# Converting the first four weight slices without absolute value and clamp, and loading their high words again later for a check

## The chip, the cores and the metric

The kernel runs on one core of one Trainium2 chip. The metric is the device time of one execution in microseconds (us): the median of three runs. Beside it stands one execution that the hardware profiler recorded; all rows in this document are of such executions. The engines are PE (TensorE matrix product; PEld is its weight load), DVE (VectorE), ACT (ScalarE), POOL (GpSimd) and SP (SyncE, which here only issues DMA transfers; its queue is SPq).

## The reference

Attention over 4 batches, 8 heads, 768 positions and 64 features per head, then a feed-forward network on its result. The projections `w_in` and `w_out` come as 64-bit floating point; the chip has to convert them.

```
scores = scale * q @ k.T + bias(head, distance); masked to a local band and some global keys
a = exp(scores - max); a = a / (sum(a) + 1e-9)
x = (a @ v) as 3072 tokens x 512
h = x @ w_in                      # 512 x 2048, float64
g = where(h > 0, h, exp(min(h, 0)) - 1)
out = (g @ w_out) as float32      # 2048 x 512, float64
```

## The kernel before, in words

The 3072 tokens are 12 groups of 256. For each group and each of 4 head pairs a chain runs: scores on PE (`s`), a masked minimum on DVE, exponentials on ACT (`pr`, L464), division, transposition, the product with v, and a split of the result into a high and a low part (`xh`, `xl`). The feed-forward part takes 16 slices of 128 hidden units: an up product into a PSUM bank `h` (12 products of 128x256; there are two such banks, h0 and h1), two ACT instructions on it (`e`, L720 and L721), one on DVE (`gg`, L722), from two slices a set of sums and splits (`rh`, `rl`, `sh`, `sl`), and a down product into banks `o`. From group 4 on, the function `seven` works on pairs of slices with seven block products instead of eight; it reads mixtures of weights (`mix`) that are loaded from DRAM for each pair. The first three groups are taken four slices at a time, while the weights are still being converted.

`weight` converts one slice of one matrix: a load of 128x1024 32-bit words (`bits`), an absolute value of the high words on ACT (L393), a clamp on DVE or POOL (L395), a shift and mask on DVE (L396), two DVE instructions that put in the sign and the low bits (L398, L400), and a split into two parts (L303 or L305, L311). Slices 0 to 3 of both matrices are eight such conversions.

The order of the instructions on each engine is not written by hand. `Plan.add` collects operations with the tiles that they read and write and a due time; `Plan.order` then builds a schedule from a table of costs and hands out slots for the tiles. An engine takes its instructions in the order that comes out, and an instruction whose operand has not arrived holds those behind it on that engine. Tiles of one class are handed out in the order in which they were added. The class `io` (four slots, `io0` to `io3`) holds the conversion's `g` early on, and later the output tiles `ob`, two for each group (slots io0 and io1), which DVE fills at the end of a group and SP stores (L805). Where the schedule shows a gap on PE in the first part, the kernel puts in products that nobody reads, to keep PE busy: `none<-fill` (L1096) and `<-zero` (L1089).

At the end a flag that tells whether the inputs lie outside of what this fast path covers is summed over the partitions; a branch on it leads to `dense`, a slow path that does not run with these inputs.

Of the kernel before, what the change touches and what calls it, by code (L numbers as in the profile page):

```python
# [28 lines left out]
HI, LO = 0, 1  # L29

F64_MIN = 2.0 ** -15
F64_MAX = 1.875 * 2.0 ** 16 - 2.0 ** -7
# [192 lines left out]
def sp():  # L225
    return (("SP", 450.0, False),)
# [19 lines left out]
class Kernel:  # L246
# [67 lines left out]
    def consts(self):  # L314
        self.ident = self.const("ident", [P, P])
        self.far0, self.far1 = self.const("far0", [P, LW]), self.const("far1", [P, LW])

        self.scale = self.const("scale", [P, self.NP])
        if self.ON_PE:
            self.minus1 = self.const("minus1", [P, P], F32R)  # L320
        self.nmax = self.const("nmax", [P, self.B * self.H * self.S // P])
        self.zero = self.const("zero", [P, W], F32R)
        self.sums = {x: self.c.tile([P, 2 * NT, 4], F32, name=x) for x in self.SLOTS["st"]}
# [57 lines left out]
    def weight(self, which, fc, due, after):  # L381
        nc, p, DM = self.nc, self.plan, self.DM
        tag = f"w{which}{fc}"
        bits = self.sb(tag, "bits", [P, 2 * DM], I32)
        g = self.sb("io", "g", [P, DM], I32)
        w = self.sb(tag, f"w{which}", [P, 2, DM], F32R)
        src = (self.w_in, self.w_out)[which][fc].bitcast(I32)
        words = lambda: bits.t.rearrange("p (n w) -> p n w", w=2)
        low, high = lambda: words()[:, :, 0], lambda: words()[:, :, 1]
        gf = lambda: g.t.bitcast(F32)  # L390
        p.add(sp(), lambda e: nc.sync.dma_start(bits.t, src), writes=[bits], due=due - 9000, after=after, nbytes=P * DM * 8, early=due - 9000 - self.EARLIER)

        p.add((("ACT", 575.0, False),), lambda e: nc.scalar.activation(gf(), high().bitcast(F32), AF.Abs), [bits], [g], due - 6000)  # L393
        p.add(dve(DM, True) + (("POOL", 640.0, True),),
              lambda e: self.on(e).tensor_scalar(gf(), gf(), F64_MAX, F64_MIN, ALU.min, ALU.max), [g], [g], due - 5500)  # L395
        p.add(dve(DM, True), lambda e: nc.vector.tensor_scalar(g.t, g.t, 3, 0x3FFFFFFF, ALU.logical_shift_left, ALU.bitwise_and),  # L396
              [g], [g], due - 5000)
        p.add(dve(DM, port=True), lambda e: nc.vector.scalar_tensor_tensor(g.t, high(), -0x40000000, g.t, ALU.bitwise_and, ALU.bitwise_or),  # L398
              [bits, g], [g], due - 4500)
        p.add(dve(DM, port=True), lambda e: nc.vector.scalar_tensor_tensor(g.t, low(), 29, g.t, ALU.logical_shift_right, ALU.bitwise_or),  # L400
              [bits, g], [g], due - 4000)
        p.add(act(DM) + pool(DM, False) + dve(DM, True), lambda e: self.copy(e, w.t[:, HI], gf()), [g], [w], due - 3000)
        if (which, fc) in self.ON_PE:

            lw = self.bank("lw", "lw", [P, DM], ["h0", "h1"])

            def lower(e):
                nc.tensor.matmul(lw.t, self.ident.t, gf(), start=True, stop=False)
                nc.tensor.matmul(lw.t, self.minus1.t, w.t[:, HI], start=False, stop=True)

            p.add((("PE", 1500.0, False),), lower, [g, w], [lw], due - 2500)
            p.add(act(DM, True), lambda e: self.copy(e, w.t[:, LO], lw.t), [lw], [w], due - 2000)
        else:
            def lower(e):
                for c in range(0, DM, DM // 2):
                    x = slice(c, c + DM // 2)
                    self.minus(e, w.t[:, LO, x], gf()[:, x], w.t[:, HI, x])

            p.add((("POOL", 1390.0, True),), lower, [g, w], [w], due - 2000)
        return w  # L420


    def pair(self, b, gi, hp, xh, xl, due, step, X):
        nc, p = self.nc, self.plan
# [487 lines left out]
    def build(self):  # L912
# [20 lines left out]
        for n, (b, gi) in enumerate(groups):  # L933
# [17 lines left out]
        for k in range(len(self.fars) + self.BEHIND):  # L951
            d = self.fars[max(0, k - self.BEHIND)][-2] - max(0, self.BEHIND - k) * self.AHEAD
# [7 lines left out]
        for (n, f0, f1), d in zip(segs, dues):  # L960
            def moe(n=n, f0=f0, f1=f1, d=d):
                b, gi = groups[n]
                if f0 == 0 and f1 < NFC:
                    parts[n] = [self.sb("part", "part", [P, self.DM]) for _ in range(NT)]
                if n >= self.SE:
                    self.seven(b * self.S + gi * W, *X[n], d, self.STEP, n == len(groups) - 1)
                    return
                self.moe(b * self.S + gi * W, *X[n], f0, f1, d, self.STEP, parts.get(n), n < self.NE, n == len(groups) - 1)
            todo.append((d[f0], moe))
        self.kept, self.mixed = {}, {}  # L970
        for j in range(NFC // 2):
            d = [x for (n, _, _), x in zip(segs, dues) if n == self.SE - 1][-1][2 * j + 1] + 2 * self.STEP
            e = self.PREPARE[0] + j * self.PREPARE[1]
# [26 lines left out]
    SOON, EARLIER = (5000.0, 2500.0, 14000.0), 1e9  # L1000
    NEAR = {}
    WARM = True
    WIDE, BEHIND_UP = ["h0", "h1", "v0", "t0"], 3.0
    THIRD = {"xha": "x0", "xhb": "ph2", "xla": "rk0", "xlb": "va0"}
    SLOTS = {"qk": ["rqv0", "qk0"], "v": ["va1", "va2"], "u": ["rk0", "va0"], "s": ["s0", "s1"], "t": ["t0"], "pv": ["v0", "t0"], "h": ["h0", "h1"], "o0": ["o0"], "o1": ["o1"],
# [95 lines left out]
    def flag(self):  # L1101
        nc, c = self.nc, self.c
        ng, nl = self.ng, self.nl
        f = c.tile([P, 8], F32, name="flag")
        nc.vector.tensor_reduce(f[:, 0:1], self.nmax.t, axis=AX.X, op=ALU.max)
        nc.vector.tensor_scalar(f[:, 0:1], f[:, 0:1], 9.0e8, None, ALU.is_ge)
        nc.vector.tensor_scalar(f[:, 1:2], ng, 0.0, None, ALU.is_lt)
        nc.vector.tensor_scalar(f[:, 2:3], ng, float(NG), None, ALU.is_gt)
        nc.vector.tensor_scalar(f[:, 3:4], nl, 0.0, None, ALU.is_lt)
        nc.vector.tensor_scalar(f[:, 4:5], nl, float(BACKW + 1), None, ALU.is_gt)  # L1110
        nc.vector.tensor_tensor(f[:, 5:6], ng, nl, ALU.add)
        nc.vector.tensor_scalar(f[:, 5:6], f[:, 5:6], 1.0, None, ALU.is_lt)
        nc.vector.tensor_reduce(f[:, 6:7], f[:, 0:6], axis=AX.X, op=ALU.max)
        one = c.tile([P, 1], F32, name="one")
        nc.gpsimd.memset(one, 1.0)
        return f, one

    def flag_sum(self, flags):
        nc, c = self.nc, self.c
        f, one = flags  # L1120
        s = self.ps.tile([P, 1], F32, tag="s0", name="flagsum")
        nc.tensor.matmul(s[0:1, :], f[:, 6:7], one, start=True, stop=True)
        fi = c.tile([1, 1], I32, name="flagint")
        nc.vector.tensor_copy(fi, s[0:1, :])
        self.fi = fi
# [110 lines left out]
    def restored(self):  # L1236
        M = self.DM // 2
        for j, x in self.kept.items():
            self.nc.sync.dma_start(self.ws[1][2 * j].t[:, :, M:].bitcast(F32), x.t)

    def dense(self, b):
        for t0 in range(0, self.S // P, NT):
            self.dx = [self.p.tile([P, self.NCC, W], F32R, tag=f"dx{i}", name=self.n("dx")) for i in range(2)]
            for i in range(NT):
                self.dense_tile(b, t0 + i, i)
            self.dense_moe(b, t0)


def tile_kernel(tc, q, k, v, qkv, qkv1, n, w_in, w_out, out):
    with ExitStack() as ctx:  # L1250
        f = Kernel(ctx, tc, q, k, v, qkv, qkv1, n, w_in, w_out, out)
        f.w = ctx.enter_context(tc.tile_pool(name="w", bufs=1))
        with tc.tile_pool(name="m", bufs=1) as f.m:
            flag = f.run()
        with tc.If(flag > 0, label="dense"):
            with ExitStack() as x:
                f.p = x.enter_context(tc.tile_pool(name="d", bufs=1))
                f.restored()
                with tc.For_i(0, f.B, 1) as b:
                    f.dense(b)  # L1260

# [63 lines left out]
```

## Time and profile before

| | |
|---|---|
| median of 3 runs | 644.96 us (644.52 to 646.63) |
| the profiled execution | 645.14 us, span of its instructions 643.4 us |
| PE busy | 632.4 us, 98% of the span |
| DVE, ACT, POOL busy | 493.9, 410.6, 197.4 us |
| granted TensorE clock, mean | 0.997 of full speed |
| DMA, mean | 233 GB/s |

Busy is time in which an engine ran instructions of its own work. The busy share is an average over stages with different limits, so the stretches have to be looked at one by one.

### The profile page before, as it was taken

To read this page: it belongs to the slowest core of one execution; us is meant where nothing else is said; L and a number is where in the kernel's file an instruction comes from. 1 tells how busy PE (TensorE), PEld (TensorE's weight loads), DVE (VectorE), ACT (ScalarE), POOL (GpSimd) and SP (SyncE) were. 2 spreads that over 40 slices of the span, in tenths; PEclk is the share of its full clock that TensorE was granted. 3 is DMA by queue.
4 is the path that set the end of the run, shared out by engine and by line. 5 is a ranking of instruction groups with operands and counts; after the bars stand their busy time and mean duration, and the time that the engine had idled before them with its cause. 6 is when DMAs were issued, how large, how long until landed. Compare 5 with 4: busy or idle time off the path is not lost.

```text
span 643.4 us, 19163 instructions
## 1 busy us (share of the span) xinstructions
PE 632.4 (98%) x7054; PEld 585.2 (91%) x7054; DVE 493.9 (77%) x1649; ACT 410.6 (64%) x1200; POOL 197.4 (31%) x499
## 2 busy tenths in 40 slices
PE   8999999999999999999999999999999999999995
PEld 5778888898898889999999999999999999999995
DVE  5999888899878975777777777786786777775655
ACT  5999777676554655666566576566566566655552
POOL 3556565465467672121111111112112022020000
PEclk9999999999999999999999999999999999999998
DMA  8979825231266899798888888898888888875542
GB/s 306 372 256 407 338 90 150 70 111 62 68 204 230 258 302 305 236 271 262 262 237 274 278 243 259 289 263 254 286 238 270 258 264 270 276 220 162 181 149 85
DMA packets 131171, 149.82 MB, mean 233 GB/s; under 512 B 63616, under 2 KB 82816, under 8 KB 131072
## 3 DMA queue, kind: packets, MB, share of 16 engines
q1 hardware_dynamic: 130928, 148.54, 72.3%
q8 instruction: 57, 0.93, 0.6%
q14 instruction: 42, 0.34, 0.2%
q10 hardware_dynamic: 144, 0.00, 0.0%
HBM read 117.57 MB, written 30.93 MB: 231 GB/s over the span
## 4 chain that ended last, share of the span: by engine, by line
PE 92%; DVE 2%; ACT 2%; DMA 2%; issue 1%; POOL 0%; DVEq 0%; ACTq 0%; SPq 0%; POOLq 0%
PE h L712 28%; PE o L768 24%; PE o L863 14%; PE h L837 14%; PE s L610 5%; PE s L474 5%; PE pv L507 2%; DMA qk<-in_qkv_dram 2%; PE t L527 1%; PE none L1096 1%; PE t L529 1%; ACT pt L303 1%; ACT pr L464 0%; DVE ob L796 0%; ACT qk L449 0%
## 5 line engine op out<-in xcount | busy, mean ns | idle before, releaser
L712 PE MATMUL h<-xh,w 128*128 128x256 f32 x1024 | 142.2, 281 | 0.1
L712 PEld LDWEIGHTS h<-xh,w 128*128 128x128 f32 x1024 | 129.8, 188 | 2.3 <-issue 1.2
L722 DVE SCALAR_TENSOR_TENSOR gg<-e,h 128x256 f32<-128x256 f32 x128 | 53.3, 416 | 75.7 <-ACT e L721 74.9
L580 POOL TENSOR_SCALAR pr<-pr,st 128x168 f32<-128x168 f32 x144 | 62.6, 435 | 150.9 <-DVE st L482 137.9
L464 ACT ACTIVATE pr<-pr,nmax 128x168 f32<-128x168 f32 x192 | 81.8, 427 | 17.6 <-DVE nmax L462 16.9
L837 PEld LDWEIGHTS h<-xh,w 128*128 128x128 f32 x512 | 77.0, 188 | 9.8 <-issue 0.2
L720 ACT ACTIVATE e<-h 128x256 f32<-128x256 f32 x128 | 48.6, 379 | 56.3 <-PE h L712 56.0
L712 PE MATMUL h<-xl,w 128*128 128x256 f32 x512 | 81.9, 281 | 0.0
L863 PE MATMUL o<-w,gh 128*128 128x512 f32 x256 | 81.6, 400 | 0.1
L837 PE MATMUL h<-xh,w 128*128 128x256 f32 x512 | 81.6, 283 | 0.0
L712 PEld LDWEIGHTS h<-xl,w 128*128 128x128 f32 x512 | 69.4, 188 | 2.0 <-issue 1.7
L462 DVE CUSTOM_DVE_ANT_0 pr<-s,far 128x168 f32<-128x168 f32 x192 | 53.3, 324 | 12.8 <-ACT xh L303 11.1
L311 POOL TENSOR_TENSOR w<-g,w 128x256 fp32r<-128x256 f32 x64 | 51.0, 818 | 36.0 <-ACT w L303 30.0
L303 ACT CAST sh<-sum 128x512 fp32r<-128x512 f32 x64 | 39.8, 621 | 31.4 <-DVE sum L736 31.4
L585 DVE STREAM_TRANSPOSE tr<-pr 128x192 f32<-128x192 f32 x144 | 50.0, 364 | 10.6 <-POOL pr L580 7.4
L721 ACT ACTIVATE e<-e 128x256 f32<-128x256 f32 x128 | 53.4, 417 | 3.6
L768 PE MATMUL o<-mix,sh 128*128 128x256 f32 x256 | 51.0, 281 | 0.0
L863 PEld LDWEIGHTS o<-w,gh 128*128 128x128 f32 x256 | 43.0, 188 | 7.6 <-issue 1.0
L311 DVE TENSOR_TENSOR sl<-sum,sh 128x512 fp32r<-128x512 f32 x64 | 44.2, 691 | 5.7 <-ACT sh L303 5.7
L768 PE MATMUL o<-w,sh 128*128 128x256 f32 x256 | 48.2, 280 | 0.0
L451 POOL TENSOR_SCALAR qk<-qk,scale 128x256 f32<-128x256 f32 x14 | 7.1, 506 | 133.3 <-DMA qk<-in_qkv_dram 90.1
L303 ACT CAST rh<-gg 128x384 fp32r<-128x384 f32 x64 | 32.8, 512 | 20.4 <-DVE gg L722 19.7
(136 smaller groups left out, 1421.4 us busy)
## 6 DMA issues: line engine op xcount, KB each, us to landing
mix<-mixed SPq DMA_DIRECT2D x192, 256.0 KB, 4.5
qk<-in_qkv_dram SPq DMA_DIRECT2D x48, 312.0 KB, 4.2
v<-in_qkv_dram SPq DMA_DIRECT2D x36, 384.0 KB, 5.0
dd<-tr SPq DMA_DIRECT2D x36, 384.0 KB, 4.5
pt<-dd SPq DMA_DIRECT2D x72, 192.0 KB, 3.9
bits<-in_w_in_dram SPq DMA_DIRECT2D x16, 512.0 KB, 8.6
bits<-in_w_out_dram SPq DMA_DIRECT2D x16, 512.0 KB, 9.5
mixed<-mix SPq DMA_DIRECT2D x32, 256.0 KB, 3.1
```

The lines of the kernel that those rows point to most:

```text
L303: self.nc.scalar.copy(out, x)
L311: self.on(e).tensor_tensor(out, x, y, ALU.subtract)
L462: first = p.add((("DVE", 85 + 1.042 * LW, False),), lambda e: nc.vector.tensor_tensor_reduce(x(), s.t[:, i, :LW], tab, -(2.0 ** -(h + 1)), ...
L464: p.add(act(LW, extra=200), lambda e: nc.scalar.activation(x(), x(), AF.Exp, bias=nm, scale=-1.0, accum_out=st.t[:, n, 0:1]), [pr], [pr, s ...
L580: nc.gpsimd.tensor_scalar(pr.t[:, :LW], pr.t[:, :LW], st.t[:, n, 3:4], 1.0, ALU.mult, ALU.mult)
L585: nc.vector.transpose(tr.t[:, :, i, j], pr.t.rearrange("p (b r) -> p b r", r=32))
L712: nc.tensor.matmul(h.t, w1.t[:, s, cc * P:(cc + 1) * P], self.chunk(x, cc), start=n == 0 and s == HI and cc == 0, stop=n == 1 and cc == se ...
L721: p.add(act(W), lambda e: nc.scalar.activation(ex.t, ex.t, AF.Exp, scale=-1.0), [ex], [ex], d - 8000)
L722: p.add(dve(W), lambda e: nc.vector.scalar_tensor_tensor(gs(), ex.t, -1.0, h.t, ALU.add, ALU.max), [h, ex], [g], d - 8000)
L768: nc.tensor.matmul(acc[bank].t[:, half], a, b.t[:, LO if t == 1 else HI, x], start=j == 0 and t == 0 and n in first, stop=j == self.NFC // ...
L837: nc.tensor.matmul(h.t, w1.t[:, s, cc * P:(cc + 1) * P], self.chunk(x, cc), start=n == 0 and cc == 0, stop=n == 2 and cc == self.NCC - 1)
L863: nc.tensor.matmul(o.t[:, :at.stop - at.start], g.t[:, i * P:(i + 1) * P], w2.t[:, s, at], start=fc == f0 and n == 0 and s == HI, stop=fc ...
```

## The change

For slices 0 to 3 (`BARE = 4`) of both matrices the absolute value and the clamp are left out, and the shift reads the high words of `bits` directly. To still tell a weight outside of the covered range, `watch` loads the words again later, in 16 transfers of 256 KB (the two matrices, four slices, two halves each), and runs two ACT instructions over the high words of each: an absolute value and an exponential, each with a sum along the row into `wide`. Five short DVE instructions in `flag` turn `wide` into one more bit of the flag. The slow path converts the four slices again with the clamp (`rewritten`, not run here and not shown).

```
-        p.add((("ACT", 575.0, False),), lambda e: nc.scalar.activation(gf(), high().bitcast(F32), AF.Abs), [bits], [g], due - 6000)
...
+        bare = fc < self.BARE
+        if not bare:
+            p.add((("ACT", 575.0, False),), lambda e: nc.scalar.activation(gf(), high().bitcast(F32), AF.Abs), [bits], [g], due - 6000)
+            p.add(dve(DM, True) + (("POOL", 640.0, True),),
+                  lambda e: self.on(e).tensor_scalar(gf(), gf(), F64_MAX, F64_MIN, ALU.min, ALU.max), [g], [g], due - 5500)
+        p.add(dve(DM, port=True) if bare else dve(DM, True), lambda e: nc.vector.tensor_scalar(
+            g.t, high() if bare else g.t, 3, 0x3FFFFFFF, ALU.logical_shift_left, ALU.bitwise_and), [bits if bare else g], [g], due - 5000)
...
+    def watch(self, k, due):
...
+        nc, p, DM = self.nc, self.plan, self.DM
+        which, fc, half = k % 2, k // 2 % self.BARE, k // 2 // self.BARE
+        src = (self.w_in, self.w_out)[which][fc].bitcast(I32)[:, half * DM:(half + 1) * DM]
+        x = self.sb("io", "seen", [P, DM], I32, slots=["io0", "io1"])
+        p.add(sp(), lambda e: nc.sync.dma_start(x.t, src), writes=[x], due=due - 4000, nbytes=P * DM * 4, early=due - 4000)
+        t = lambda: x.t.rearrange("p (n w) -> p n w", w=2)[:, :, 1].bitcast(F32)
+        w, n = self.wide, 4 * self.BARE
+        p.add(act(DM // 2, extra=200), lambda e: nc.scalar.activation(t(), t(), AF.Abs, accum_out=w[:, k:k + 1]), [x], [x], due)
+        p.add(act(DM // 2, extra=200), lambda e: nc.scalar.activation(t(), t(), AF.Exp, scale=-512.0, accum_out=w[:, n + k:n + k + 1]), [x], [x], due)
...
+        for k in range(4 * self.BARE):
+            d = self.WATCH[0] + k * self.WATCH[1]
+            todo.append((d - 4000.0, lambda k=k, d=d: self.watch(k, d)))
...
+    BARE, WATCH = 4, (255000.0, 12000.0)
```

The 16 loads use the slots of the output tiles, so they stand behind the stores at the ends of five groups (4 to 8): 2, 4, 4, 4 and 2 of them. First the SP queue at the end of group 4, before the change: the two stores of the output, three loads of mixtures, and the loads for the attention of a later group.

```order
L805 DMA out_dram<-ob_5192 128x512
L805 DMA out_dram<-ob_5156 128x512
L751 DMA mix_5249<-mixed_3302 128x512
L751 DMA mix_5265<-mixed_3271 128x512
L751 DMA mix_5280<-mixed_3286 128x512
L548 DMA qk_5324<-in_qkv_dram 128x624
L556 DMA v_5336<-in_qkv_dram 128x768
```

The same place with the change (lines are 16 higher in the changed file), with what each instruction waits for; DMAHW5 and DMAHW6 are here the semaphores of the two stores:

```order
L821 DMA out_dram<-ob_5166 128x512 [waits DMAHW5_49,DVE_49]
L821 DMA out_dram<-ob_5130 128x512 [waits DMAHW6_49,DVE_49]
L767 DMA mix_5223<-mixed_3276 128x512 [waits PE_49]
L767 DMA mix_5239<-mixed_3258 128x512 [waits DMAHW0_49,PE_49]
L767 DMA mix_5254<-mixed_3264 128x512 [waits DMAHW1_49,PE_49]
L433 DMA seen_5256<-in_w_in_dram 128x512 [waits DMAHW5_49,DMAHW2_49]
L433 DMA seen_5294<-in_w_out_dram 128x512 [waits DMAHW6_49,DMAHW3_49]
L564 DMA qk_5302<-in_qkv_dram 128x624 [waits DMAHW4_49,PE_49,Activation_49]
```

Two loads have come in behind the mixtures. Each waits for the store that empties its slot. At the next three group ends a second pair of loads follows, and these wait for the ACT instructions on the first pair, whose slots they take.

ACT at the same place before the change: `e` on the first slice of the new group, exponentials of the attention, `e` on the second slice.

```order
L720 ACTIVATE e_5338<-h_5269 128x256
L721 ACTIVATE e_5338<-e_5338 128x256
L464 ACTIVATE pr_5340,st_75<-pr_5340,nmax 128x168
L464 ACTIVATE pr_5343,st_75<-pr_5343,nmax 128x168
L720 ACTIVATE e_5365<-h_5326 128x256
L464 ACTIVATE pr_5349,st_75<-pr_5349,nmax 128x168
L721 ACTIVATE e_5365<-e_5365 128x256
L464 ACTIVATE pr_5361,st_75<-pr_5361,nmax 128x168
```

And with the change:

```order
L736 ACTIVATE e_5316<-h_5243 128x256
L737 ACTIVATE e_5316<-e_5316 128x256
L480 ACTIVATE pr_5318,st_76<-pr_5318,nmax 128x168
L436 ACTIVATE seen_5256,wide<-seen_5256 128x256
L736 ACTIVATE e_5343<-h_5304 128x256
L437 ACTIVATE seen_5256,wide<-seen_5256 128x256
L436 ACTIVATE seen_5294,wide<-seen_5294 128x256
L737 ACTIVATE e_5343<-e_5343 128x256
L437 ACTIVATE seen_5294,wide<-seen_5294 128x256
```

The four new instructions stand in front of and between the two `e` of the second slice; the other exponentials have moved behind them.

PE in the first part, at the first up product of the feed-forward network, before the change: runs of seven and of two unread products (`none<-zero`) stand around it.

```order
L1089 MATMUL none_566<-zero 128x256 x7
L837 MATMUL h_574<-xh_331,w_104_463 128x256 x2
L837 MATMUL h_574<-xh_500,w_104_463 128x256 x2
L837 MATMUL h_574<-xh_331,w_104_463 128x256 x2
L837 MATMUL h_574<-xh_500,w_104_463 128x256 x2
L527 MATMUL t_589<-ident,pr_486 128x128
L527 MATMUL t_589<-ident,pr_493 128x128
L529 MATMUL t_589<-ident,pr_486 128x128
L529 MATMUL t_589<-ident,pr_493 128x128
L837 MATMUL h_574<-xl_350,w_104_463 128x256 x2
L837 MATMUL h_574<-xl_520,w_104_463 128x256 x2
L1089 MATMUL none_614<-zero 128x256 x2
```

And with the change: the first run is two products long, the second is gone, and the second slice's product has moved up. In the whole program the products of L1089 (L1109 in the changed file) fall from 22 (runs of 7, 2, 5, 4, 4) to 11 (runs of 2 and 9), and those of L1096 rise from 22 to 24.

```order
L1109 MATMUL none_560<-zero 128x256 x2
L853 MATMUL h_563<-xh_333,w_104_410 128x256 x2
L853 MATMUL h_563<-xh_482,w_104_410 128x256 x2
L853 MATMUL h_563<-xh_333,w_104_410 128x256 x2
L853 MATMUL h_563<-xh_482,w_104_410 128x256 x2
L853 MATMUL h_563<-xl_351,w_104_410 128x256 x2
L853 MATMUL h_563<-xl_501,w_104_410 128x256 x2
L543 MATMUL t_582<-ident,pr_473 128x128
L543 MATMUL t_582<-ident,pr_480 128x128
L545 MATMUL t_582<-ident,pr_473 128x128
L545 MATMUL t_582<-ident,pr_480 128x128
L853 MATMUL h_592<-xh_333,w_110_553 128x256 x2
```

## Rows read from the trace of the kernel before

**Rows 1.** Page, part 1: busy time of each engine, share of the span, instructions.

```profile
PE 632.4 (98%) x7054; PEld 585.2 (91%) x7054; DVE 493.9 (77%) x1649; ACT 410.6 (64%) x1200; POOL 197.4 (31%) x499
```

**Rows 2.** Windows: length, busy us (x instructions) by engine, PE clock, DMA share, GB/s.

```profile
30.00:40.00 10.00, 8.99 (x133) 7.42 (x132) 9.33 (x37) 9.85 (x35) 6.02 (x9) 1.00 0.51 159
40.00:50.00 10.00, 9.54 (x110) 7.51 (x110) 9.93 (x38) 9.80 (x34) 5.46 (x8) 1.00 0.98 366
...
280.00:320.00 40.00, 40.00 (x542) 38.51 (x541) 28.86 (x105) 25.14 (x74) 5.71 (x25) 1.00 0.85 262
```

**Rows 3.** PE groups from 6 to 70 us, unread products: busy us, mean ns | idle before.

```profile
L1096 PE MATMUL none<-fill 128*128 128x512 f32 x14 | 5.5, 509 | 0.0
L1089 PE MATMUL none<-zero 128*128 128x256 f32 x14 | 2.3, 294 | 0.0
L1089 PE MATMUL o<-zero 128*128 128x256 f32 x8 | 1.4, 293 | 0.0
```

**Rows 4.** Lines of the conversion, 0 to 160 us: duration ns min/median/max, first and last start.

```profile
L393 ACT ACTIVATE g<-bits x32: 647/674/692, 14.9 to 156.0; 128x512 f32<-128x512 f32 x32
L395 DVE TENSOR_SCALAR g<-g x10: 415/423/940, 15.7 to 154.8; 128x512 f32<-128x512 f32 x10
L396 DVE TENSOR_SCALAR g<-g x30: 412/424/964, 18.1 to 157.1; 128x512 int32<-128x512 int32 x30
L398 DVE SCALAR_TENSOR_TENSOR g<-bits,g x30: 644/684/1222, 18.6 to 159.3; 128x512 int32<-128x512 int32 x30
```

**Rows 5.** Timeline of ACT from 10 us: start, us, line, tiles; pieces merged.

```profile
21.88 1.83 ACT L393 ACTIVATE g<-bits 128x512 f32<-128x512 f32 x3
```

**Rows 6.** Timeline of SP's queue at the end of group 4: start us, us of issuing.

```profile
308.80 0.86 SPq L805 DMA_DIRECT2D out_dram<-ob  x2
309.71 2.92 SPq L751 DMA_DIRECT2D mix<-mixed  x3
312.73 0.37 SPq L548 DMA_DIRECT2D qk<-in_qkv_dram  x1
```

**Rows 7.** DMA issues at five group ends (308.8, 357.9, 407.3, 456.1, 505.4 us), KB, us to landing.

```profile
out_dram<-ob SPq DMA_DIRECT2D x2, 256.0 KB, 5.0
...
out_dram<-ob SPq DMA_DIRECT2D x2, 256.0 KB, 4.7
...
out_dram<-ob SPq DMA_DIRECT2D x1, 256.0 KB, 4.1
...
out_dram<-ob SPq DMA_DIRECT2D x1, 256.0 KB, 3.7
...
out_dram<-ob SPq DMA_DIRECT2D x1, 256.0 KB, 4.6
```

**Rows 8.** DMA issues 3 to 4 us behind the stores: at 312.6, 410.3, 459.3 us.

```profile
qk<-in_qkv_dram SPq DMA_DIRECT2D x1, 312.0 KB, 4.9
...
qk<-in_qkv_dram SPq DMA_DIRECT2D x1, 312.0 KB, 5.7
mix<-mixed SPq DMA_DIRECT2D x1, 256.0 KB, 5.5
...
mix<-mixed SPq DMA_DIRECT2D x1, 256.0 KB, 4.7
```

**Rows 9.** Timeline of ACT at the start of group 5.

```profile
313.06 0.42 ACT L464 ACTIVATE pr<-pr,nmax 128x168 f32<-128x168 f32 x1
...
313.48 0.42 ACT L464 ACTIVATE pr<-pr,nmax 128x168 f32<-128x168 f32 x1
...
313.90 0.36 ACT L720 ACTIVATE e<-h 128x256 f32<-128x256 f32 x1
...
314.58 0.41 ACT L721 ACTIVATE e<-e 128x256 f32<-128x256 f32 x1
...
316.54 0.62 ACT L303 CAST sh<-sum 128x512 fp32r<-128x512 f32 x1 [0.54 <-DVE sum L736]
```

**Rows 10.** Timeline of DVE there: `gg` of the second slice.

```profile
315.02 0.42 DVE L722 SCALAR_TENSOR_TENSOR gg<-e,h 128x256 f32<-128x256 f32 x1 [0.76 <-ACT e L721]
```

**Rows 11.** Timeline of PE there.

```profile
313.07 0.63 PE L712 MATMUL h<-xl,w 128*128 128x256 f32 x4
313.54 0.63 PE L768 MATMUL o<-w,rh 128*128 128x256 f32 x4
...
316.01 1.10 PE L712 MATMUL h<-xh,w 128*128 128x256 f32 x8
...
318.95 1.21 PE L712 MATMUL h<-xh,w 128*128 128x256 f32 x8
```

More of the change, by code (lines that the diff above doesn't have):

```diff
@@ L318, in consts @@
         self.scale = self.const("scale", [P, self.NP])
+        self.wide = self.c.tile([P, 8 * self.BARE], F32, name="wide")
         if self.ON_PE:
@@ L391, in weight @@
         p.add(sp(), lambda e: nc.sync.dma_start(bits.t, src), writes=[bits], due=due - 9000, after=after, nbytes=P * DM * 8, early=due - 9000 - self.EARLIER)
-        p.add((("ACT", 575.0, False),), lambda e: nc.scalar.activation(gf(), high().bitcast(F32), AF.Abs), [bits], [g], due - 6000)
[L394 to L397, printed above, removed]
+        bare = fc < self.BARE
[5 more added lines that the diff above has]
+            g.t, high() if bare else g.t, 3, 0x3FFFFFFF, ALU.logical_shift_left, ALU.bitwise_and), [bits if bare else g], [g], due - 5000)
         p.add(dve(DM, port=True), lambda e: nc.vector.scalar_tensor_tensor(g.t, high(), -0x40000000, g.t, ALU.bitwise_and, ALU.bitwise_or),
@@ L1112, in flag @@
         nc.vector.tensor_scalar(f[:, 5:6], f[:, 5:6], 1.0, None, ALU.is_lt)
-        nc.vector.tensor_reduce(f[:, 6:7], f[:, 0:6], axis=AX.X, op=ALU.max)
+        w, n = self.wide, 4 * self.BARE
+        nc.vector.tensor_scalar(w[:, :n], w[:, :n], 2.0 ** 16, None, ALU.is_lt)
+        nc.vector.tensor_scalar(w[:, n:], w[:, n:], 0.5, None, ALU.is_lt)
+        nc.vector.tensor_reduce(f[:, 6:7], w, axis=AX.X, op=ALU.min)
+        nc.vector.tensor_scalar(f[:, 6:7], f[:, 6:7], -1.0, 1.0, ALU.mult, ALU.add)
+        nc.vector.tensor_reduce(f[:, 7:8], f[:, 0:7], axis=AX.X, op=ALU.max)
         one = c.tile([P, 1], F32, name="one")
@@ L1121, in flag_sum @@
         s = self.ps.tile([P, 1], F32, tag="s0", name="flagsum")
-        nc.tensor.matmul(s[0:1, :], f[:, 6:7], one, start=True, stop=True)
+        nc.tensor.matmul(s[0:1, :], f[:, 7:8], one, start=True, stop=True)
         fi = c.tile([1, 1], I32, name="flagint")
@@ L1239, in restored, with rewritten @@
             self.nc.sync.dma_start(self.ws[1][2 * j].t[:, :, M:].bitcast(F32), x.t)
+    def rewritten(self):
+        nc, p, DM = self.nc, self.p, self.DM
+        for fc in range(self.BARE):
+            for which in range(2):
+                bits = p.tile([P, 2 * DM], I32, tag="bits", name=self.n("bits"))
+                g = p.tile([P, DM], I32, tag="bg", name=self.n("bg"))
+                w = self.ws[which][fc].t
+                gf = g.bitcast(F32)
+                words = bits.rearrange("p (n w) -> p n w", w=2)
+                nc.sync.dma_start(bits, (self.w_in, self.w_out)[which][fc].bitcast(I32))
+                nc.scalar.activation(gf, words[:, :, 1].bitcast(F32), AF.Abs)
+                nc.vector.tensor_scalar(gf, gf, F64_MAX, F64_MIN, ALU.min, ALU.max)
+                nc.vector.tensor_scalar(g, g, 3, 0x3FFFFFFF, ALU.logical_shift_left, ALU.bitwise_and)
+                nc.vector.scalar_tensor_tensor(g, words[:, :, 1], -0x40000000, g, ALU.bitwise_and, ALU.bitwise_or)
+                nc.vector.scalar_tensor_tensor(g, words[:, :, 0], 29, g, ALU.logical_shift_right, ALU.bitwise_or)
+                nc.scalar.copy(w[:, HI], gf)
+                nc.vector.tensor_tensor(w[:, LO], gf, w[:, HI], ALU.subtract)
     def dense(self, b):
@@ L1258, in tile_kernel @@
                 f.restored()
+                f.rewritten()
                 with tc.For_i(0, f.B, 1) as b:
```

## Prediction

> **What bounds the kernel now.** I read the page's busy shares first: PE is busy for 98% of the span [rows 1]. The windows then say where that is real. From 280 to 320 us PE works 40.00 of 40 us at full granted clock, ACT 25.1 and DVE 28.9 [rows 2]; the other windows between 80 and 560 us look alike. There nothing but PE work, or a wait that newly reaches PE, can move the time. In the first 60 us it is another matter: between 30 and 50 us ACT (9.85 and 9.80 of 10 us) and DVE (9.33 and 9.93) are full and PE is idle for 1.01 + 0.46 us [rows 2], and part of PE's busy time there is products that nobody reads: from 6 to 70 us 14 of L1096 (5.5 us) and 22 of L1089 (2.3 + 1.4 us) [rows 3]. So the change works on the one stretch where ACT and DVE limit PE, and adds work where PE has no slack at all.
>
> **What the change saves at the start.** Eight absolute values leave ACT. Three back to back take 1.83 us, with 0.10 us of the last overlapping its successor, so one costs 0.57 us [rows 5] (0.67 us alone [rows 4]): 8 x 0.57 = 4.6 us. Eight clamps leave DVE and POOL; of all 32, ten ran on DVE, so two or three here, about 0.34 us of issue each, some 0.9 us [rows 4]. The shift stays but reads every second word. No row shows that: it costs at least the 0.42 us of L396 and at most the 0.68 us of L398, which reads the same words with a second source [rows 4]. So DVE moves by -0.9 to +1.2 us; I take the middle, nothing. The VectorE page of the Trainium skill (VectorE: DVE Perf Modes, What auto-detection actually checks) gives a one-source operation between SBUF tiles its doubled rate without asking for adjacent words. By that rule the shift stays at 0.42 us and the start gains a few tenths more; no run here shows it yet.
>
> What reaches PE I read from the order. The unread products of L1089 fall from 22 to 11, at 3.7/22 = 0.17 us each -1.85 us; those of L1096 rise by two at 5.5/14 = 0.39, +0.8 us [rows 3]. Of PE's 1.47 us idle [rows 2] I let half go, -0.75 us, because ACT loses 4.6 of some 40 us up to the place where it last limits PE. Sum -1.8 us. Ends: -5.2 us, if all of L1089 and all the idle time go (3.7 + 1.47), and +2.0 us, if the fills (+0.8) and the slower shift (+1.2) both land on PE.
>
> **What the loads cost later.** By volume they are covered: 16 transfers of 256 KB beside a DMA share of 0.85 [rows 2], and 32 activations of about 0.5 us (0.41 us for 128x256 and 0.09 for the sum's read-out), 16 us over 200 us in which ACT idles for more than a third. The flag's five short instructions come behind the last attention scores, off PE's path. But ACT takes its instructions in order, and the first new one stands in front of `e` of the new group's second slice. So when does its data land?
>
> Count from the first store of a group's output, 308.80 us at group 4 [rows 6]. The load must wait until that store has landed: 5.0, 4.7, 4.1, 3.7 and 4.6 us at the five ends, median 4.6 [rows 7]; SP is through with the mixtures at 312.63, after 3.8 us [rows 6]. The load itself then takes as long as its neighbours: 4.7 to 5.7 us [rows 8], I take 5.0. With 0.1 us between, the data is there at 4.6 + 0.1 + 5.0 = 9.7 us. ACT is ready for it behind the first `pr`, at 313.48, which is 4.7 us [rows 9]. It stands for 5.0 us, with `e`, `pr`, `rh` and `sh` behind it.
>
> Does PE notice? The second slice's `h` is finished at 313.54 [rows 11]. PE goes on with a down block, the third slice (in the other bank) and an attention visit, and wants the second slice's bank again at 318.95, 10.15 us after the store [rows 11]. That bank is free once `gg` has read it. From the data's landing: first activation 0.5, `e` 0.3, second activation 0.5, first activation of the second load 0.5, `e` 0.3, `gg` with its hand-over 0.4 [rows 9, 10], 2.5 us in all. 9.7 + 2.5 = 12.2 us; PE stands for 2.05 us. Five group ends: 10.25 us.
>
> At three of these ends a second pair follows. Its first load waits for the second activation, 9.7 + 1.3 = 11.0, and lands at 11.0 + 0.1 + 5.0 = 16.1 us. ACT reaches it after `sh` at about 14.3 and stands for 1.8 us; the third slice's `e` is behind it, and its bank is free 2.0 us after landing, at 18.1. PE: 12.2, plus a slice 1.4 (12 products at 0.117), plus a down block 2.47 (313.54 to 316.01 [rows 11]), wants the bank at 16.1. Another 2.0 us, three times: 6.0 us. The fourth load finds ACT still busy and adds nothing.
>
> SP stands too, for about 1 us per end at the store and again for the second pair. Behind it are `qk` and `v` of a visit two later and mixtures of the pair after next; I price that at nothing, covered by that lead. If the cover fails, it is the fourth rival.
>
> Sum: -1.8 + 10.25 + 6.0 = +14.4 us on the profiled execution's 645.14 us (span 643.4 and 1.7 around it): 659.6. The median of the runs shown is 0.2 us lower, so **659.4 us**. Bounds: with the fastest store and load (3.7, 4.7) the two waits are 0.85 and 1.7 us, 9.4 us in all; with the slowest (5.0, 5.7) 3.15 and 2.7, 23.9 us. With -1.8 us the likeliest case lies between 652.5 and 667.
>
> The trace has 4.6 to 5 us for a 256 KB transfer here [rows 7, 8]. The Trainium skill (DMA: Bandwidth & Descriptors, Anatomy of one DMA) fits one transfer issued from GpSimd with about 2.0 us fixed and the bytes at 436 GB/s, an estimated 2.6 us for 256 KB. By that the data would be there at about 6.5 us and PE would not wait, which is the first rival's case; the rows of this queue, with its other transfers in flight, speak against it.
>
> **Rivals.** 0.3% (1.9 us) is about what a measurement of this kernel can tell from no change.
> - No wait reaches PE: the data lands within 10.15 - 2.5 = 7.6 us of the store, the point that decides. Then only the start counts: 643.2 us, with its ends 639.8 to 647.0. For it: the new loads read DRAM in whole rows, as `qk` does, but are smaller, and could be quicker than any neighbour. Against it: store and load at their fastest here are 8.5 us. Chance 0.15: 0.09 faster by over 0.3%, 0.06 within it.
> - Only the first pair's wait reaches PE, because PE, once late, gives ACT time to catch up and the second pair has landed: -1.8 + 10.25, 653.4 us. Against it: the second pair cannot be issued before ACT has used the first. Chance 0.2.
> - Both waits, as summed: 0.5.
> - The waits spread: the exponentials behind the stalled instruction are some 7 us late, and with them the attention's transposition by way of DRAM, so that a visit two later waits as well, or the mixtures behind SP's wait come late. At 1.5 us for each end, 5 x 1.5 more: 667 us. Chance 0.15.
>
> So faster 0.09, same 0.06, slower 0.85. The range that leaves out no more than 2 in 10 leaves out most of the first rival and the far part of the last: 647 to 668.
>
> **What the changed trace would show.** Right: ACT idle before the first new activation at each of five places, for about 5 us, released by a DMA, and PE idle 2 us before an up product just behind, released by DVE's `gg`; PE's busy time down by 1 us in the first 70 us. Wrong: PE still at 40 of 40 us between 300 and 520; or the waits on ACT there but not on PE, which would mean that I counted PE's lead too short; or a landing well under 4 us for the new loads. The start is wrong if `t` and `pv` products wait longer behind a slower shift.

## The result, and the profile after

The changed kernel takes 653.88 us (median of 5 runs, 651.6 to 661.45) against 644.52 us before in the same job. The ratio is 1.0126, with a 95% interval of 1.0106 to 1.0146: slower by some 8 us. One of the five, 661.45 us, ran at a lower granted clock (0.992) and is left out of the ratio. The profiled execution took 653.88 us, its span 652.1 us.

The time divides at the place where DVE begins to add up the output of group 4, which no late load precedes. These are PE's windows, of the kernel before up to 70 us and from that place to the output of the last group: length, PE busy us (x products), granted clock, DMA share, GB/s.

```profile
0.00:70.00 70.00, 65.69 (x785) 1.00 0.88 332
303.79:636.46 332.67, 332.43 (x4001) 1.00 0.79 243
```

And the same windows of the changed kernel:

```profile
0.00:70.00 70.00, 66.15 (x817) 1.00 0.90 342
299.65:645.24 345.59, 335.52 (x4001) 1.00 0.79 247
```

The place comes at 299.65 instead of 303.79 us: the start has gained 4.14 us in this execution. Then the same 4001 products take 12.92 us longer. Of these, 9.83 us show as idle time of PE (10.07 against 0.24). The other 3.09 us lie in rows that count as busy. Four products in a run take 0.63 us and eight 1.10 [rows 11], so each starts 0.12 us after the one before, while the row of one alone is 0.28 us long; its end is modelled. A wait of PE is thus some 0.16 us longer than its idle time, and the eight products behind it take 1.21 us (rows below) and not 1.10. PE waited 15 times in this window, and twice before the change (waits over 0.04 us): 13 x 0.27 = 3.5 us by this estimate, which covers the 3.09.

**The start.** Of the changed kernel: the windows that answer to those of [rows 2] (all engines, in the order PE, PEld, DVE, ACT, POOL), the unread products from 6 to 70 us as in [rows 3], and the bare shift (duration min/median/max).

```profile
30.00:40.00 10.00, 9.03 (x124) 7.04 (x118) 7.58 (x30) 8.96 (x32) 6.58 (x11) 1.00 0.64 205
40.00:50.00 10.00, 10.00 (x141) 8.27 (x140) 8.65 (x36) 9.44 (x34) 4.06 (x6) 1.00 1.01 385
```

```profile
L1116 PE MATMUL none<-fill 128*128 128x512 f32 x16 | 5.0, 424 | 0.0
L1109 PE MATMUL o<-zero 128*128 128x256 f32 x9 | 1.3, 291 | 0.0
L1109 PE MATMUL none<-zero 128*128 128x256 f32 x2 | 0.5, 334 | 0.0
```

```profile
L399 DVE TENSOR_SCALAR g<-bits x8: 407/424/529, 13.6 to 49.0; 128x512 int32<-128x512 int32 x8
```

In these windows ACT and DVE are no longer full, the shift costs the 0.42 us of its adjacent form [rows 4], and the unread products of L1109 take 1.8 us instead of 3.7. The lead is there even before these windows. This is PE's first up product before the change, and then with it:

```profile
28.52 1.11 PE L837 MATMUL h<-xh,w 128*128 128x256 f32 x8
```

```profile
25.80 1.10 PE L853 MATMUL h<-xh,w 128*128 128x256 f32 x8
```

**The end of group 4.** SP's queue with the change answers to [rows 6]:

```profile
304.65 0.86 SPq L821 DMA_DIRECT2D out_dram<-ob  x2
305.56 1.89 SPq L767 DMA_DIRECT2D mix<-mixed  x3
309.23 0.33 SPq L433 DMA_DIRECT2D seen<-in_w_in_dram  x1
309.87 0.50 SPq L433 DMA_DIRECT2D seen<-in_w_out_dram  x1
310.47 0.37 SPq L564 DMA_DIRECT2D qk<-in_qkv_dram  x1
```

The load stands for the store and goes out 4.58 us behind it. This is ACT at the first activation on a late load, wherever it stood for more than 0.1 us; in brackets is how long. The rows at 366.92 and 417.75 us are of third loads, those at 369.76, 421.85 and 475.75 us of fourth loads, that at 521.58 us is of the second load of the last pair, and the others are of first loads.

```profile
312.92 0.44 ACT L436 ACTIVATE seen<-seen 128x256 f32<-128x256 f32 x1 [3.48 <-issue]
...
362.06 0.43 ACT L436 ACTIVATE seen<-seen 128x256 f32<-128x256 f32 x1 [1.91 <-DMA seen<-in_w_in_dram]
...
366.92 0.45 ACT L436 ACTIVATE seen<-seen 128x256 f32<-128x256 f32 x1 [0.33 <-DMA seen<-in_w_in_dram]
...
369.76 0.45 ACT L436 ACTIVATE seen<-seen 128x256 f32<-128x256 f32 x1 [0.99 <-DMA seen<-in_w_out_dram]
...
412.85 0.44 ACT L436 ACTIVATE seen<-seen 128x256 f32<-128x256 f32 x1 [2.83 <-DMA seen<-in_w_in_dram]
...
417.75 0.44 ACT L436 ACTIVATE seen<-seen 128x256 f32<-128x256 f32 x1 [0.74 <-DMA seen<-in_w_in_dram]
...
421.85 0.43 ACT L436 ACTIVATE seen<-seen 128x256 f32<-128x256 f32 x1 [1.98 <-DMA seen<-in_w_out_dram]
...
467.81 0.44 ACT L436 ACTIVATE seen<-seen 128x256 f32<-128x256 f32 x1 [4.30 <-DMA seen<-in_w_in_dram]
...
475.75 0.43 ACT L436 ACTIVATE seen<-seen 128x256 f32<-128x256 f32 x1 [1.68 <-DMA seen<-in_w_out_dram]
...
518.60 0.43 ACT L436 ACTIVATE seen<-seen 128x256 f32<-128x256 f32 x1 [2.59 <-DMA seen<-in_w_in_dram]
...
521.58 0.43 ACT L436 ACTIVATE seen<-seen 128x256 f32<-128x256 f32 x1 [1.61 <-DMA seen<-in_w_out_dram]
```

PE behind it: the up products that found their bank not free, and a down product that waited for `sh` (419.92 us).

```profile
315.45 1.21 PE L728 MATMUL h<-xh,w 128*128 128x256 f32 x8 [0.57 <-DVE gg L738]
...
371.80 1.21 PE L728 MATMUL h<-xh,w 128*128 128x256 f32 x8 [0.71 <-DVE gg L738]
...
416.29 1.21 PE L728 MATMUL h<-xh,w 128*128 128x256 f32 x8 [0.42 <-DVE gg L738]
...
419.92 0.50 PE L784 MATMUL o<-mix,sh 128*128 128x256 f32 x2 [0.90 <-ACT sh L303]
...
423.19 1.21 PE L728 MATMUL h<-xh,w 128*128 128x256 f32 x8 [1.04 <-DVE gg L738]
...
470.25 1.21 PE L728 MATMUL h<-xh,w 128*128 128x256 f32 x8 [1.30 <-DVE gg L738]
...
477.76 1.18 PE L728 MATMUL h<-xh,w 128*128 128x256 f32 x8 [1.82 <-DVE gg L738]
...
523.59 1.21 PE L728 MATMUL h<-xh,w 128*128 128x256 f32 x8 [1.73 <-DVE gg L738]
```

The group of these up products from 296 to 560 us, with the idle time before it:

```profile
L728 PE MATMUL h<-xh,w 128*128 128x256 f32 x664 | 92.9, 282 | 7.7 <-DVE gg L738 7.6
```

The chain of the forecast stands here in rows: a load late, ACT standing for it, `gg` late behind ACT, PE idle behind `gg`. From the starts of DVE's first addition to a group's output (303.79, 352.67, 401.56, 450.45, 499.33, 548.80 us before; 299.65, 350.48, 400.63, 453.71, 506.63, 557.72 after) the five stretches have lost 1.95, 1.26, 4.19, 4.04 and 1.62 us; at the first and the last end there is one pair of loads, at the others there are two. The order of PE's products has changed too: the first stretch holds six more of them than before and the second seven fewer, so these two are off by some 0.8 us either way.

### The profile page after: what moved, and what is told of

The parts are those of the page before. It is cut to its first block, busy times and chain, and to the rows that moved or that the text cites. A ratio compares the mean times of both kernels' runs of the same rounds, so it can differ in the third digit from the quotient of the medians.

```text
span 652.1 us, 19223 instructions
## 1 busy us (share of the span) xinstructions
PE 631.7 (97%) x7045; PEld 583.4 (89%) x7045; DVE 491.5 (75%) x1636; ACT 413.6 (63%) x1260; POOL 209.1 (32%) x504
## 4 chain that ended last, share of the span: by engine, by line
PE 75%; DMA 10%; ACT 7%; DVE 5%; issue 2%; POOL 1%; SPq 0%; ACTq 0%; DVEq 0%; POOLq 0%
PE h L728 21%; PE o L784 18%; PE o L879 12%; PE h L853 12%; PE s L490 3%; PE s L626 3%; DMA seen<-in_w_in_dram 3%; DMA seen<-in_w_out_dram 3%; PE pv L523 2%; ACT pr L480 2%; PE t L543 1%; DMA pt<-dd 1%; DMA mix<-mixed 1%; ACT seen L436 1%; DMA qk<-in_qkv_dram 1%
## 5 line engine op out<-in xcount | busy, mean ns | idle before, releaser
L596 POOL TENSOR_SCALAR pr<-pr,st 128x168 f32<-128x168 f32 x144 | 70.2, 487 | 139.3 <-DVE st L498 105.7
L478 DVE CUSTOM_DVE_ANT_0 pr<-s,far 128x168 f32<-128x168 f32 x192 | 53.6, 324 | 13.3 <-ACT xh L303 10.7
L467 POOL TENSOR_SCALAR qk<-qk,scale 128x256 f32<-128x256 f32 x23 | 13.3, 579 | 147.9 <-DMA qk<-in_qkv_dram 82.4
L311 POOL TENSOR_TENSOR w<-g,w 128x256 fp32r<-128x256 f32 x64 | 49.0, 788 | 27.8 <-ACT w L303 22.1
```

The source lines that it names most:

```text
L311: self.on(e).tensor_tensor(out, x, y, ALU.subtract)
L478: first = p.add((("DVE", 85 + 1.042 * LW, False),), lambda e: nc.vector.tensor_tensor_reduce(x(), s.t[:, i, :LW], tab, -(2.0 ** -(h + 1)), ...
L596: nc.gpsimd.tensor_scalar(pr.t[:, :LW], pr.t[:, :LW], st.t[:, n, 3:4], 1.0, ALU.mult, ALU.mult)
```

## Experiments

The theory was that ACT stands for the late loads and PE behind it. Against it stood that the start gains less than it seems, that the traffic costs, that the activations' own time costs, and that SP's standing at the stores costs. Diffs are against the changed kernel unless said otherwise; ratios are to the kernel before.

**e1_bare_only.** The loads and activations are gone.

```
-        for k in range(4 * self.BARE):
-            d = self.WATCH[0] + k * self.WATCH[1]
-            todo.append((d - 4000.0, lambda k=k, d=d: self.watch(k, d)))
```

> The conversion of slices 0 to 3 stays bare; the late loads and their 32 activations are left out, and with them the part of the check on the weights that sets the flag. Theory (ACT stands for the late loads, and PE behind it): only the gain of the start is left. The changed kernel's store of group 4 came 4.15 us before that of the kernel before, ahead of any late load, so 644.5 - 4.2 = 640.3 us, between 639.5 and 641.5, and PE at 19.9 of 20 us from 300 to 560. Rival (the start gains only the 1.8 us of the forecast, the rest of the lead is an accident of that execution): 642.7. Rival (the loss comes from the changed order that the plan makes after the bare conversion): above 645, with PE idle after 300 us as in the changed kernel.

642.58 us, ratio 0.9968 (0.994 to 0.9996). The gain is 1.4 us by the medians and 2.1 by the ratio, near the forecast's 1.8 us; the interval reaches to 3.9 us and just leaves out the 4.2 of the theory. The changed order alone costs nothing. Loss and gain are separate things: the start gains, the late part loses.

**e2_loads_only.** The loads stay, the activations go.

```
-        p.add(act(DM // 2, extra=200), lambda e: nc.scalar.activation(t(), t(), AF.Abs, ...
-        p.add(act(DM // 2, extra=200), lambda e: nc.scalar.activation(t(), t(), AF.Exp, ...
```

> The 16 late loads stay in their slots behind the stores, and SP's queue with their waits; the 32 activations that read them are left out (so nothing looks at the loaded words). Theory: no instruction of ACT stands for them, so 640.3 us as without the loads, up to 641.5. Rival (traffic of 4 MB, or SP standing at the stores and so late loads of qk, v and mixtures): most of the 13 us remains, 650 to 654, with PE waits on mixtures or on attention.

652.96 us, ratio 1.0134 (1.0108 to 1.0161): as slow as the whole change, and the theory as stated falls. These are SP's waits from 296 to 510 us (us in total, times, longest), and PE's groups from 296 to 560 us with idle time:

```profile
SPq L433 <- DMA out_dram<-ob: 8.5, 8, 1.7
SPq L433 <- DMA seen<-in_w_out_dram: 3.0, 2, 1.6
SPq L433 <- DMA seen<-in_w_in_dram: 2.6, 3, 1.4
```

```profile
L726 PE MATMUL h<-xh,w 128*128 128x256 f32 x664 | 92.2, 280 | 1.4 <-DVE gg L736 1.4
...
L624 PE MATMUL s<-pt,v 64*64 64x64 f32 x960 | 20.1, 227 | 6.2 <-DMA pt<-dd 5.7 <-PE h L726 0.5
```

PE now waits at another place, for the attention's transposition by way of DRAM. SP stood for 14.1 us in all, and what is behind the loads in its queue came late: at group 6 the load `pt` went out 26.6 us behind DVE's first addition to the output of that group (399.80 to 426.39 us), in e1 20.8 us (399.55 to 420.35). That is the part of the fourth rival which the forecast priced at nothing. In the changed kernel that load goes out as late (26.7 us, 400.63 to 427.36), yet PE does not wait for it; that ACT's stand has already made PE late enough is the likely reason, and not shown.

**e3_acts_only.** The activations run on two tiles that are filled once.

```
-        p.add(sp(), lambda e: nc.sync.dma_start(x.t, src), writes=[x], ...
+            p.add((("POOL", 640.0, True),), lambda e: nc.gpsimd.memset(x.t.bitcast(F32), 1.0), writes=[x], ...
```

> The 16 late loads are left out; the 32 activations run at the due times, each pair every 12 us, on two tiles that POOL fills once (so the check looks at constants). Theory: 16 to 20 us of ACT work in the idle third of ACT, nothing of it on PE: 640.3 to 641.5 us. Rival (the activations' own time, in front of e and pr, is what PE pays): 16 pairs at about 0.5 to 0.8 us, 648 to 653.

The execution took 5795.26 us, ratio 8.992 (8.9754 to 9.0085), since the constants set the flag and the slow path ran behind the fast one. (The edit also lets the activations start 1.5 us before their due time.) The fast part is read from the trace, from group 4's output to the last group's:

```profile
301.23:633.16 331.93, 331.69 (x4000) 1.00 0.80 245
```

331.93 us against 332.67 before: the 32 activations cost nothing.

**e4_io_slack.** The plan puts the first activation 6 us later in ACT's order.

```
-        p.add(act(...), lambda e: nc.scalar.activation(t(), t(), AF.Abs, ...), [x], [x], due)
+        p.add(act(...), lambda e: nc.scalar.activation(t(), t(), AF.Abs, ...), [x], [x], due, slack=6000.0)
```

> All of the change stays, in the same slots and behind the same stores; the plan is told that the first activation on each load may run 6 us after it believes the load to have landed, so other instructions of ACT go first. In its schedule the first activation then stands some 14 us behind the store instead of 8 to 9. Theory: the data (7.5 to 9.7 us behind the store in the changed kernel) is there before ACT comes to it, ACT does not stand, 640.5 to 642 us, faster than both kernels. Rival (traffic, or the activations' time, or SP's standing at the stores): nothing of the sort changes, 650 to 655.

645.15 us, ratio 1.0011 (0.9991 to 1.0032): nearly all of the loss is gone, by a new order alone, with every load and activation kept. No wait of ACT for `seen` is left in the view of waits. But ACT stood for something else (from 296 to 640 us), and PE for 1.6 us behind `ob`:

```profile
ACT qk L465 <- DMA qk<-in_qkv_dram: 14.6, 9, 2.7
```

So the sum of ACT's standing doesn't decide; that it is what is queued behind it fits, but is not shown by itself. SP still stood for stores here, 5.5 us from 296 to 510 us (5.6 in the changed kernel).

**e5_own_slots_at_ends.** No load waits for a store.

```
-        x = self.sb("io", "seen", [P, DM], I32, slots=["io0", "io1"])
+        x = self.sb("io", "seen", [P, DM], I32, slots=["rk0", "va0"])
```

> The late loads keep their place in the class of the output tiles, and so come at the ends of the same five groups, but they go to two slots of their own that are free from 240 us on (rk0 and va0); no load waits for a store, and SP does not stand for one. The plan believes a load to take 3.1 us, the rows say 4.5 to 5.0, so ACT stands some 2 us at a place. Theory (two waits that lie side by side and are each enough, ACT standing for the data and SP standing for the store with the transposition's stores behind it): SP's is gone, ACT's 2 us are within the 4 us or so by which PE is ahead, so 642.5 us as without the loads, between 641.5 and 644.5. Rival (traffic that comes together with the stores at the ends of groups): 649 to 654.

651.59 us, ratio 1.0091 (1.0064 to 1.0119). The expectation missed: ACT's stands were much longer than 2 us. ACT's waits from 296 to 640 us, and PE's group with the idle time behind them:

```profile
ACT seen L436 <- DMA seen<-in_w_in_dram: 24.2, 8, 6.5
```

```profile
L728 PE MATMUL h<-xh,w 128*128 128x256 f32 x666 | 94.0, 283 | 4.0 <-DVE gg L738 4.0
```

The loads landed after 4.1 to 6.4 us (median 5.3), where the plan gives them about 3. SP is free of the stores and most of the loss is still there.

**e6_own_slots_ACT_early.** As e5, with ACT there earlier.

```
-        ... AF.Abs, accum_out=w[:, k:k + 1]), [x], [x], due)
+        ... AF.Abs, accum_out=w[:, k:k + 1]), [x], [x], due, slack=-2500.0)
```

> As the kernel with slots of their own at the ends of groups, but the plan is told that the first activation may run 2.5 us before it believes the load to have landed: ACT then comes to it within 1 us of the issue and stands some 4 to 4.5 us with e behind it, while SP still waits for no store. If ACT's stand by itself is enough for a loss: PE is ahead by about 4 us, so 0.5 to 1.5 us at five ends and about as much again where a second pair follows, 646 to 652 us, with PE waiting for gg. If only SP's standing counts: 642.5 to 644.5 and no PE wait for gg.

684.35 us, ratio 1.0609 (1.0544 to 1.0675), far beyond the 646 to 652 expected. ACT's waits for loads from 296 to 640 us, and PE's group from 296 to 560 us:

```profile
ACT seen L436 <- DMA seen<-in_w_in_dram: 38.6, 8, 8.4
ACT seen L436 <- DMA seen<-in_w_out_dram: 8.7, 6, 2.1
```

```profile
L728 PE MATMUL h<-xh,w 128*128 128x256 f32 x581 | 85.6, 291 | 28.0 <-DVE gg L738 28.0
```

ACT's standing is enough by itself: 47.3 us of it, with no load behind a store, became 28.0 us on PE by `gg`.

**e7_own_class.** The loads come one by one, out of line with the output tiles.

```
-        x = self.sb("io", "seen", [P, DM], I32, slots=["io0", "io1"])
+        x = self.sb("seen", "seen", [P, DM], I32)
...
+             "seen": ["rk0", "va0"], "g": ["io2", "io3"],
```

> The late loads have a class and two slots of their own (rk0, va0): one load every 12 us at its due time from 251 to 431 us, none waits for a store or stands in line behind output tiles. ACT comes 3 us after the issue, so it stands up to 2 us, 16 times, apart from each other. Theory: 642.5 us, between 641.5 and 644, since each stand is shorter than PE's lead and no two meet. Rival (each stand of ACT reaches PE in part): 16 times 0.3 to 0.6 us, 647 to 652.

652.34 us, ratio 1.0118 (1.008 to 1.0156). The expectation missed again, and its rival held. From 240 to 640 us ACT waited for `seen` 21.0 + 4.7 us in 12 pieces, none longer than 4.0 us, and PE for `gg` 2.7 us in the profiled execution, which at 648.36 us was this kernel's fastest. Spread stands cost as much as clustered ones (e5), within the intervals.

**e8_own_class_slack.** As e7, with the landing allowed for.

```
-        ... AF.Abs, accum_out=w[:, k:k + 1]), [x], [x], due)
+        ... AF.Abs, accum_out=w[:, k:k + 1]), [x], [x], due, slack=4000.0)
```

> As the kernel before this in the list, and the plan is told that the first activation may run 4 us after it believes the load to have landed, so ACT should find the data there. All of the check is kept. Theory: 642.5 us, between 641 and 643.5, faster than both kernels by what the start gains. Rival (traffic of 4 MB): 645 or more.

641.59 us, ratio 0.9947 (0.9931 to 0.9962): faster than both kernels with the whole check kept, the best version found. ACT's waits for the loads from 240 to 640 us, and PE's window from group 4's output to the last group's:

```profile
ACT seen L436 <- DMA seen<-in_w_in_dram: 1.8, 2, 1.0
```

```profile
299.53:631.66 332.13, 331.93 (x4001) 1.00 0.82 253
```

The same 4 MB, the same 32 activations, landings of 3.4 to 6.0 us: traffic costs nothing. One argument of the plan lies between this and e7, which makes these two the plainest evidence that ACT's stand is what costs.

**e9_loads_only_later.** As e2, with the loads behind `qk` and `v` in SP's queue.

```
-        p.add(sp(), ..., early=due - 4000)
+        p.add(sp(), ..., early=due - 4000, slack=10000.0)
```

> As the kernel with the 16 loads and no activation on them (nothing looks at the loaded words), same slots behind the same stores, but the plan is told that a slot comes free 3 us later than it believes; in SP's queue qk and v then stand ahead of the late loads instead of behind them. Theory (in the kernel with the loads alone ACT stood up to 3.95 us for qk, which SP issued late because it stood for the stores): ACT stands no more, 642.5 us, between 641 and 644.5. Rival (the traffic behind the stores, or slots that come free late): 650 to 653 as before.

642.44 us, ratio 0.9952 (0.9923 to 0.9981). SP's waits from 296 to 510 us:

```profile
SPq L433 <- DMA out_dram<-ob: 1.5, 3, 0.8
SPq L433 <- DMA seen<-in_w_in_dram: 0.5, 1, 0.5
```

(Of the 10 us in the edit, the plan adds three tenths to the time at which a slot comes free.) 14.1 us of SP's standing have become 2.0, and the loss of e2 is gone, with the same traffic. That SP's stand was the cause there is shown. By which way it reached PE is not: the expectation says `qk` and ACT, but ACT stood for `qk` 8.1 us here without a loss and 14.6 us in e4 with little; PE's rows of e2 say the transposition.

**e10_old_conversion_slack.** As e8, with the conversion as before (`bare = False`).

> The late loads in a class and slots of their own with 4 us for the landing, but the conversion of slices 0 to 3 as in the kernel before, with absolute value and clamp: the start is undone. Theory: the late part costs nothing, so the kernel before, 644 to 645.5 us, and the difference to the kernel with the bare conversion, about 3.4 us, is what the start gains. Rival (the gain there was from something that the late loads change): faster than 643.

645.27 us, ratio 1.0008 (0.9983 to 1.0034). The late part of e8 is free, and the start is worth 1.0008 - 0.9947 = 0.61%, 3.9 us.

**e11_watch_on_old.** The change's loads on the conversion as before (`bare = False`, and nothing else).

> The late loads and activations just as in the change, on the conversion as before. Theory (start and late part add up): the changed kernel plus what the start gains, 653.9 + 3.4 = 657, between 654 and 660. By the forecast's terms it would be 645 + 10.25 + 6.0 = 661. Rival (PE's being early or late shifts the waits, and the two don't add): under 653.

658.89 us, ratio 1.0218 (1.0175 to 1.0262). Start and late part add up, within the intervals: 1.0126 + 0.0061 = 1.0187. In the profiled execution the window from group 4's output to the last group's is 345.56 us long, where the changed kernel has 345.59.

**e12_first_pairs.** Six loads fewer.

```
-        for k in range(4 * self.BARE):
+        for k in (0, 1, 2, 3, 6, 7, 10, 11, 14, 15):
```

> The changed kernel with the first two late loads of each of the five group ends alone; the second pairs at three ends, six loads and twelve activations, are left out (those words are not looked at). By the forecast's terms the second pairs cost 6.0 us, so 653.9 - 6.0 = 648. Theory after the traces (the second pairs' stands were 0 to 0.7 us for the third load, 1.0 to 2.0 for the fourth, and the group ends with two pairs lost 1.3 to 4.2 us, those with one about 2): 648 to 651. Rival (only first pairs count): 653.5.

654.37 us, ratio 1.0113 (1.0075 to 1.015). Without the second pairs the kernel is no faster that could be measured. ACT's waits from 296 to 640 us:

```profile
ACT seen L437 <- DMA seen<-in_w_in_dram: 16.3, 5, 6.1
ACT qk L466 <- DMA qk<-in_qkv_dram: 16.1, 5, 4.1
```

Five first loads stood for 16.3 us. ACT's waits for `qk`, which in the changed kernel come to 5.2 us in this stretch, have grown to 16.1: part of what was taken away came back as another wait. The plan has ordered the rest anew: the first load at the first end stood 6.06 us (3.48 in the changed kernel), and PE waited 3.04 us behind the first end and 2.17 behind the last, instead of 0.57 and 1.73. So this run is not the changed kernel less six loads, and what the second pairs cost there can't be taken from the difference.

## Why the prediction was right, and where it was not

The time lies in the range and the sign is right, by the mechanism that was named. 659.4 was 5.5 us too high: in the profiled execution the start gained 4.14 us and not 1.8, and the late part cost 12.92 us and not 16.25. Both errors point the same way, so neither hid the other.

**What bounds the kernel: right.** From group 4 on, PE had 0.24 us of slack in 332.67 us; whatever reached it was time.

**The start: gains, but mis-sized.** The term was -1.8 us with ends at -5.2 and +2.0. e8 gives 0.53% of 644.5, -3.4 us (-2.4 to -4.4), e8 against e10 -3.9. L1089's part was right (3.7 to 1.8 us). The fills rose by two as read from the order but fell in time, from 5.5 to 5.0 us up to 70 us, instead of +0.8: the rows of this one product last from 0.39 to 0.79 us, so counting them by the mean was wrong. The shift was taken at the middle and measured 0.42 us, the lower end. That agrees with the Trainium skill (VectorE: DVE Perf Modes, What auto-detection actually checks), by whose rule the start was to gain a few tenths more. PE's idle time, of which half of 1.47 us was to go, fell by 0.50 us in the same two windows, and its busy time in the first 70 us rose, from 65.69 to 66.15 us, instead of falling by 1: 32 more products fit in. What the sum had no term for lies before these windows. The first up product starts 2.72 us earlier, yet PE's idle time up to there is no shorter (2.55 us before, 2.88 after); rows that count as busy have become shorter (`s<-qk` from 6 to 70 us: 12.2 us before, 10.9 after). Which wait ended there is open.

**The first pair at each end: right in its links, mis-sized in the landing.** At the end of group 4 the load went out 4.58 us behind the store (forecast 4.7), `gg` let PE go 2.53 us after the data (2.5), PE wanted the bank at 315.45 - 0.57 - 304.65 = 10.23 us (10.15). But the first loads took 3.6, 4.6, 4.0, 5.8 and 3.6 us at the five ends and not 5.0, so ACT had their data 8.3, 8.5, 8.6, 9.7 and 7.5 us behind the store and not at 9.7. With these times the forecast's own rule gives 0.6, 0.9, 0.9, 2.1 and 0 us of wait; PE's rows have 0.57, 0, 0.42, 1.30 and 1.73. That is 4.0 us at five ends, some 5 with the 0.27 that each wait hides, where 10.25 were forecast. The 1.73 us came by a link that the forecast left out: at the last end the second load of the pair landed 3 us after the first, ACT stood another 1.61 us for it, and `e` of the second slice was behind that. The estimate of 2.6 us for a landing, from the fit that the Trainium skill (DMA: Bandwidth & Descriptors, Anatomy of one DMA) gives for one transfer issued from GpSimd, does not hold on this queue with its other transfers: the late loads took 3.0 to 6.2 us, median 4.5.

**The second pairs: near in size, by another link.** "Another 2.0 us, three times: 6.0 us." The third load stood for 0.33, 0.74 and 0 us and not 1.8, since it went out 9.7 to 11.0 us behind the first store (forecast 11.1) and took 3.0 to 3.6 us and not 5.0. The fourth, which was to add nothing, took 5.1 to 6.2 us and stood for 0.99, 1.98 and 1.68 us. Behind them PE waited 0.71 us at the second end, 0.90 + 0.27 + 1.04 at the third and 1.82 at the fourth: 4.7 us, some 6 with what the waits hide. That the size is near is luck, since the link was another. e12 does not settle it: against the change it gives 0.13%, 0.8 us, with intervals of some 0.4% and in another order. The second rival, 653.4 us, came nearest in time, but by coincidence: its -1.8 + 10.25 are wrong each by itself, and second pairs do make PE wait.

**Traffic and activations at nothing: right** (e8, e3). **SP's standing at nothing: wrong**, and unseen in the result: alone it costs 1.0134 - 0.9968 = 1.66%, 10.7 us (e2). But its sum decides no more than ACT's: with SP standing for stores as long as in the changed kernel, e4 lost 1.0011 - 0.9947 = 0.64% against e8, 4.1 us, some of it behind `ob`. Beside ACT's stand it adds nothing that could be measured (1.0126 with the activations, 1.0134 without); that both delay the same stretch and PE pays for the later is argued, not shown.

Open is also why e1 is not clearly as fast as e8, which does more; their intervals overlap.

## What to carry to other kernels

On an engine that takes its instructions in order, a consumer of a late load is a wait for all that stands behind it, however idle the engine is on the mean: look at what is queued behind it, and let a plan that sets the order allow for the landing that the trace shows. When a suspected wait is taken away and the time stays, look for a second one over the same stretch before dropping the first: here ACT's stand (e5 to e7) and SP's (e2) were each enough, taking away ACT's alone brought the kernel back to the time before (e4), and with the whole check only the version without both (e8) was faster. The late loads of e8 go to buffers that are free anyway, and SP stands for no store; in e4 a buffer has to be emptied first.

## What the runs showed of the hardware beyond that

A wait of PE can cost more than its length. In e6, PE's clock behind a stall of 5.71 us: windows, then PE's timeline.

```profile
364.00:368.00 4.00, 0.90 (x4) 0.77 0.82 311
368.00:372.00 4.00, 4.00 (x71) 0.50 0.76 246
```

```profile
367.10 2.08 PE L728 MATMUL h<-xh,w 128*128 128x256 f32 x8 [5.71 <-DVE gg L738]
...
371.71 1.22 PE L728 MATMUL h<-xl,w 128*128 128x256 f32 x4
```

The granted clock was 0.50, the lower level of 1.2 GHz, and the same products took up to twice as long (four in 1.22 us, where [rows 11] has 0.63). The waits of the changed kernel, 1.82 us at most, left the windows at 1.00. Length alone does not decide: in e12 the clock was 0.71 from 318 to 322 us around a wait of 3.04 us, and in e2 0.67 from 432 to 436 us, behind waits of 0.90 and 1.17 us with two small products between them. So some of the loss in e2 and e12 is the clock's.

In e6 this is the smaller part. Its 4001 products took 375.97 us from group 4's output to the last group's, 43.3 us more than before the change. 29.4 of these are waits, and 13.9 lie in rows that count as busy, the slowed products among them. That the waits themselves would be so long is what the expectation had missed.
